# Natural row order with 8 KB runs, a quadrant move on TensorE, and a third held value pass, in an attention kernel fed from HBM

## The chip, the cores and the metric

The kernel runs on one core of one Trainium2 chip. The metric is the device time of one execution in microseconds (us), as the median of several runs. All runs quoted here are of the fast state and ran at a granted TensorE clock of 1.00. The experiments were timed in five batches on several chips (e1 to e4, e5 to e8, e9 to e12, e13 to e16, e17 and e18), each with the kernel before in the same rounds. Its median was 1242.7 to 1245.7 us in them, so medians of two batches can be off against each other by up to 3 us. A ratio is always to the kernel before of the same rounds, and is the safer number between batches.

## The reference, cut to what matters

```python
# x: 8 rows (batch elements) of 512; caches: 8 x 8 groups x 8192 tokens x 128; 32 query heads, 4 per group; all bf16
def _A_ref(x, k_cache, v_cache, wq, wo):
    q = (x @ wq) ...                      # 8 x 32 heads x 1 x 128
    scores = einsum("bhqd,bhkd->bhqk", q, k) * 128 ** -0.5
    p = softmax(scores)
    return einsum("bhqk,bhkd->bhqd", p, v) ... @ wo
def _B_ref(x, w1, w2):
    return silu(x @ w1) @ w2
x = A_x
x = x + _A_ref(_layernorm(x), A_k_cache, A_v_cache, A_wq, A_wo)    # layer 0
x = x + _B_ref(_layernorm(x), B_w1, B_w2)
x = x + _A_ref(_layernorm(x), A_k_cache, A_v_cache, A_wq, A_wo)    # layer 1, the same caches
x = x + _B_ref(_layernorm(x), B_w1, B_w2)
```

The keys and values of both layers are the same 268 MB. The kernel keeps the transposed keys of one batch element in SBUF for layer 1, so keys are read once and values twice: 402.7 MB, of 484.8 MB in all.

## The kernel before

A planner in Python simulates the engines, fixes the order of instructions and gives each load a place in a ring of ten 512 KB cells. Every load goes out from SyncE in that fixed order, and waits there until its cell is free. A "unit" is one layer, batch element and group: four key cells are transposed by VectorE in 32x32 blocks (1.99 us a cell), TensorE makes the scores, GpSimd and VectorE find the maximum over all tokens, ScalarE takes the exponential, and TensorE multiplies four value cells.

Between layer 0 and layer 1 of one batch element there is a chain without large loads: output projection, residual, feed-forward, norm, queries. The loads that wait for it stop the stream, because layer 1 can't score before its queries exist. So the value passes of the last two units of layer 1 are held back ("held", N_DEF) and done in the next such boundary, while layer 0 of the next element is interleaved too.

```python
N_GRAN = 11; N_P = 3; N_DEF = 2; N_BD = 4; T_TURN = 1.2
...
    def load_v(b, g, P):      # 128 partitions x 4096 B, one run each
        return load_gran(f"v{b}.{g}.{P}", v_src(b, g)[P], 1)
    def v_src(b, g):
        return A_v_cache[b, g].rearrange("(P n r) d -> P n (r d)", P=4, n=128)
    def load_k(b, g, c4):
        src = A_k_cache[b, g].rearrange("(p c4 cg) d -> c4 p (cg d)", p=128, c4=4)
        return load_gran(f"k{b}.{g}.{c4}", src[c4], 1)
...
    def turns(b, g):
        new = slot(g).bitcast(U32).rearrange("p (k i c4) -> p c4 k i", i=32, c4=4)   # output in 16 B steps
        for c4 in range(4):
            kn = load_k(b, g, c4)
            def turn(kn=kn, c4=c4):
                raw = gran(kn.give).bitcast(U32).rearrange("p (k j) -> p k j", j=32)
                op(dve, lambda: dve.transpose(new[:, c4], raw), ...)
...
        def exp():
            op(act, lambda: act.activation(pt[:, :], sv, ACT.Exp, scale=SM_SCALE), ...)
...
# norm: 1/sqrt(var) as a power on GpSimd, which otherwise runs partition_all_reduce
            op(pool, lambda: pool.tensor_tensor(rstd[:, 0:nb], var[:, 0:nb], expo[:, 0:nb], ALU.pow), ...)
...
            for h in held:                       # at the boundary between the layers
                values(h)
```

## Time and profile before

| | before |
|---|---|
| time, median of 4 runs | 1244.2 us (1241.7 to 1246.8) |
| profiled span | 1245.3 us |
| DMA queue of the inputs, share of 16 engines | 98.7% |
| TensorE, VectorE, ScalarE busy | 51%, 57%, 5% |
| bandwidth on its plateau | 408 GB/s |

These are lines of the profile's page: the span, busy times, the bandwidth in 40 equal slices, packets, the queue of instruction fetches (packets, MB, share), and two groups of instructions (line, engine, operation, output and input, count, busy us, mean ns of one, idle time just before them and what ended most of it).

```profile
span 1245.3 us, 45478 instructions
PE 631.6 (51%) x20640; PEld 593.0 (48%) x20640; DVE 708.4 (57%) x1236; ACT 63.0 (5%) x202; POOL 117.0 (9%) x295
...
GB/s 362 407 398 408 337 371 408 408 408 356 393 408 408 407 371 407 407 408 399 376 409 407 407 394 373 408 408 408 371 389 408 407 407 364 410 407 408 394 339 208
DMA packets 136865, 484.80 MB, mean 389 GB/s; under 512 B 14544, under 2 KB 20448, under 8 KB 136672
...
q8 instruction: 162, 2.65, 0.9%
...
L605 DVE STREAM_TRANSPOSE kts<-ring 128x1024 uint32<-128x1024 uint32 x256 | 503.2, 1988 | 116.6 <-DMA ring<-in_A_k_cache_dram 116.4
...
L656 PE MATMUL sc<-bd,kts 128*128 128x16 bf16 x8192 | 278.2, 174 | 160.7 <-issue 53.2
```

The bandwidth row is the one to read. It lies at 408 wherever nothing disturbs it and dips once per batch element. The dip of the third batch element in stretches of 10 us (columns: length, busy us and count of each engine, granted clock, DMA share, GB/s):

```profile
434.00:444.00 10.00, 4.75 (x156) 4.45 (x156) 8.30 (x14) 0.77 (x2) 1.39 (x4) 1.00 0.99 380
444.00:454.00 10.00, 4.15 (x145) 3.90 (x141) 4.44 (x6) 0.00 (x0) 0.50 (x2) 1.00 1.02 395
454.00:464.00 10.00, 6.02 (x200) 5.72 (x201) 7.71 (x13) 0.94 (x3) 1.10 (x3) 1.00 0.95 341
464.00:474.00 10.00, 4.58 (x155) 4.26 (x151) 5.87 (x10) 0.56 (x2) 1.17 (x3) 1.00 1.02 399
```

The share of busy DMA engines stays at 0.95 or more here while the bandwidth falls. Part of the loss thus shows as packets that take longer (up to 1.2 us for one of 4096 B) and not as idle engines.

And lines of the waits view (who waited, for what; us in total, times, longest): what SyncE's queue waited for before it could issue a load, and what TensorE and GpSimd waited for.

```profile
SPq L89 <- DVE kts L605: 270.6, 146, 8.2
SPq L89 <- PE ot L733: 252.9, 246, 4.8
...
PE ot L733 <- DMA ring<-in_A_v_cache_dram: 115.7, 123, 5.6
POOL rstd L413 <- issue: 7.1, 1, 7.1
```

SyncE waits in most of the span (779 us in all by that view), and far less than that is lost: up to ten cells can be in flight, and the row stays at 408 GB/s as long as a cell comes free in time. So a wait is counted as a loss only where the bandwidth falls.

A quantity that the rest uses is the **loss**: the span less the stream time. The stream time is every packet counted at what one of its size costs on the plateau (160.3 ns for 4096 B, read from undisturbed stretches; the packets of 4 B that go along are contained in these figures and not counted again), over 16 engines. For the kernel before it is 1187.6 us of stream and 57.7 us of loss.

### The profile page before, as it was taken

Reading aid. Unit: us, or ns where it says so; the run is one execution under the profiler, and the core shown is the slowest. Engines: PE = TensorE matmul, PEld = TensorE weight load, DVE = VectorE, ACT = ScalarE, POOL = GpSimd, SP = SyncE. Lnnn points to the kernel's source line nnn. Section 1 sums busy time; section 2 is a strip of 40 time slices with the busy share of each in tenths; the row PEclk is TensorE's granted clock in tenths of the full one; section 3 lists DMA queues with packets and bytes.
Section 4 is the critical chain, followed back from the end, with each engine's and each line's share of the span. In section 5 each row is a group of like instructions: output and inputs, shape, how many; then the busy total and the mean of one; then the engine's idle time right before and its main releaser. Section 6 shows DMA issues by size and latency. Waiting matters only on the chain.

```text
span 1245.3 us, 45478 instructions
## 1 busy us (share of the span) xinstructions
PE 631.6 (51%) x20640; PEld 593.0 (48%) x20640; DVE 708.4 (57%) x1236; ACT 63.0 (5%) x202; POOL 117.0 (9%) x295
## 2 busy tenths in 40 slices
PE   2334545455554654546454554555555455454555
PEld 2333545445543544545444454544545455444554
DVE  7745466826477265764557546574556826577221
ACT  0000000000000000000000000000000000000000
POOL 1000010101010010110000100110101101011010
DMA  9999999999999999999999999999999999999995
GB/s 362 407 398 408 337 371 408 408 408 356 393 408 408 407 371 407 407 408 399 376 409 407 407 394 373 408 408 408 371 389 408 407 407 364 410 407 408 394 339 208
DMA packets 136865, 484.80 MB, mean 389 GB/s; under 512 B 14544, under 2 KB 20448, under 8 KB 136672
## 3 DMA queue, kind: packets, MB, share of 16 engines
q1 hardware_dynamic: 136672, 481.90, 98.7%
q8 instruction: 162, 2.65, 0.9%
q14 instruction: 31, 0.25, 0.1%
HBM read 481.83 MB, written 0.01 MB: 387 GB/s over the span
## 4 chain that ended last, share of the span: by engine, by line
DMA 41%; DVE 25%; issue 20%; PE 10%; SPq 2%; POOL 2%; ACT 0%; POOLq 0%; DVEq 0%
DMA ring<-in_A_k_cache_dram 24%; DVE kts L605 19%; DMA ring<-in_A_v_cache_dram 10%; DMA ring<-in_A_wq_dram 7%; PE sc L656 5%; PE ot L733 2%; SPq L312 2%; DVE sc L678 2%; DVE small L668 2%; PE misc L563 1%; POOL small L673 1%; DVE small L687 1%; POOL small L692 1%; DVE bd L640 0%; PE yt L784 0%
## 5 line engine op out<-in xcount | busy, mean ns | idle before, releaser
L605 DVE STREAM_TRANSPOSE kts<-ring 128x1024 uint32<-128x1024 uint32 x256 | 503.2, 1988 | 116.6 <-DMA ring<-in_A_k_cache_dram 116.4
L733 PE MATMUL ot<-p,ring 128*128 128x4 bf16 x8192 | 287.4, 167 | 177.0 <-DMA ring<-in_A_v_cache_dram 115.7
L656 PE MATMUL sc<-bd,kts 128*128 128x16 bf16 x8192 | 278.2, 174 | 160.7 <-issue 53.2
L733 PEld LDWEIGHTS ot<-p,ring 128*128 128x128 bf16 x8192 | 255.5, 104 | 193.6 <-DMA ring<-in_A_v_cache_dram 131.1
L656 PEld LDWEIGHTS sc<-bd,kts 128*128 128x128 bf16 x8192 | 249.8, 104 | 168.9 <-issue 56.0
L673 POOL PARTITION_ALL_REDUCE small<-small x128 | 48.1, 376 | 728.9 <-DVE small L668 631.8
L668 DVE TENSOR_REDUCE small<-sc 128x4 f32<-128x256 f32 x128 | 51.9, 406 | 107.6 <-PE sc L656 107.4
L683 ACT ACTIVATE p<-sc 128x256 bf16<-128x256 f32 x128 | 49.0, 383 | 729.6 <-DVE sc L678 729.6
L784 PE MATMUL yt<-z,ring 128*128 128x4 bf16 x1024 | 36.8, 166 | 93.1 <-DVE z L762 89.8
L692 POOL PARTITION_ALL_REDUCE small<-small x128 | 55.0, 431 | 268.4 <-DVE small L687 266.1
L784 PEld LDWEIGHTS yt<-z,ring 128*128 128x128 bf16 x1024 | 33.0, 104 | 96.2 <-issue 96.0
L563 PE MATMUL misc<-xn,ring 128*128 128x1 bf16 (+1 forms) x1152 | 36.2, 166 | 68.7 <-DMA ring<-in_A_wq_dram 62.1
L563 PEld LDWEIGHTS misc<-xn,ring 128*128 128x128 bf16 x1152 | 33.8, 104 | 71.1 <-issue 64.9
L678 DVE TENSOR_TENSOR sc<-sc,small 128x256 f32<-128x256 f32 x128 | 57.1, 447 | 18.2 <-POOL small L673 17.9
L687 DVE TENSOR_REDUCE small<-p 128x4 f32<-128x256 bf16 x128 | 51.2, 401 | 21.3 <-ACT p L683 21.0
L632 PE MATMUL qx<-qab,sel 128*128 128x4 bf16 x256 | 16.6, 169 | 54.5 <-DVE bd L640 54.5
L696 DVE RECIPROCAL small<-small 128x4 f32<-128x4 f32 x128 | 21.6, 168 | 34.6 <-POOL small L692 34.6
L632 PEld LDWEIGHTS qx<-qab,sel 128*128 128x128 bf16 x256 | 11.8, 106 | 56.5 <-DVE bd L640 56.5
L640 DVE TENSOR_TENSOR bd<-qx,mask 128x64 bf16<-128x64 f32 x128 | 27.7, 217 | 16.2 <-PE qx L632 16.0
L571 DVE CAST qtb<-misc 128x4 bf16<-128x4 f32 (+1 forms) x32 | 5.3, 166 | 54.3 <-PE misc L563 54.3
L743 DVE TENSOR_TENSOR qab<-ot,small 128x4 bf16<-128x4 f32 x64 | 10.0, 157 | 43.6 <-PE ot L733 43.4
L762 DVE TENSOR_TENSOR z<-ot,small 128x16 bf16<-128x16 f32 x64 | 10.5, 164 | 37.7 <-PE ot L755 37.7
(61 smaller groups left out, 206.3 us busy)
## 6 DMA issues: line engine op xcount, KB each, us to landing
ring<-in_A_v_cache_dram SPq DMA_DIRECT2D x512, 512.0 KB, 10.8
ring<-in_A_k_cache_dram SPq DMA_DIRECT2D x256, 512.0 KB, 10.6
ring<-in_A_wq_dram SPq DMA_DIRECT2D x72, 512.0 KB, 10.8
ring<-in_A_wo_dram SPq DMA_DIRECT2D x64, 512.0 KB, 11.0
kts<-in_A_wo_dram SPq DMA_DIRECT2D x2, 2048.0 KB, 16.9
w<-in_B_w_dram SPq DMA_DIRECT2D x2, 1792.0 KB, 14.9
ring<-in_A_x_dram SPq DMA_DIRECT2D x1, 8.0 KB
out_dram<-ring SPq DMA_DIRECT2D x1, 8.0 KB
```

The costliest lines, as they stand in the source:

```text
L563: steps.append(lambda h=h, kt=kt, c=c: pe.matmul(qp[:, h * nb:(h + 1) * nb], gran(wn[kt].give)[:, c:c + DH], xn[:, b0:b0 + nb, kt], start= ...
L605: op(dve, lambda: dve.transpose(new[:, c4], raw), reads=[res("ring", kn.give)], writes=[res("kt", g)], add=(c4 > 0))
L632: steps.append(lambda fe=fe: pe.matmul(QX[:, R * fe:R * fe + R], sel[:, fe].rearrange("p a j -> p (a j)"), qsrc, start=True, stop=True))
L656: steps.append(lambda cg=cg, fe=fe: pe.matmul(sc[:, 16 * cg:16 * cg + 16], kv[:, cg, fe // 2, fe % 2], bd[:, 16 * fe:16 * fe + 16], start= ...
L668: op(dve, lambda: dve.tensor_reduce(mxp[sm], sv.rearrange("p (k h) -> p h k", h=R), AX.X, ALU.max), reads=[res(*scr)], writes=[res("mxp", ...
L673: op(pool, lambda: pool.partition_all_reduce(mxa[sm], mxp[sm], 128, bass.bass_isa.ReduceOp.max), reads=[res("mxp", sm)], writes=[res("mxa" ...
L678: op(dve, lambda: dve.tensor_tensor(v, v, mxa[sm].unsqueeze(1).to_broadcast([128, NCH, R]), ALU.subtract), reads=[res("mxa", sm)], writes= ...
L683: op(act, lambda: act.activation(pt[:, :], sv, ACT.Exp, scale=SM_SCALE), reads=[res(*scr)], writes=[res("p", sm)])
L687: op(dve, lambda: dve.tensor_reduce(ssm[sm], pt[:, :].rearrange("p (k h) -> p h k", h=R), AX.X, ALU.add), reads=[res("p", sm)], writes=[re ...
L692: op(pool, lambda: pool.partition_all_reduce(ssa[sm], ssm[sm], 128, bass.bass_isa.ReduceOp.add), reads=[res("ssm", sm)], writes=[res("ssa" ...
L733: steps.append(lambda cg=cg, k=k: pe.matmul(ot[:, 0:R], vt[:, cg, :], pt[:, k:k + R], start=(P == 0 and cg == 0), stop=(P == 3 and cg == N ...
L784: steps.append(lambda j=j, dt=dt: pe.matmul(YT[:, dt * R:(dt + 1) * R], w[:, j, dt * 128:(dt + 1) * 128], zt[:, R * j:R * j + R], start=(g ...
```

## The change

Its intent: let keys and values come in natural order, with 8192 B per partition instead of 4096 B, so that the DMA engines pay for half as many packets. Two cells then form a pair of 1 MiB that lands and comes free at once. In natural order the probability of a token sits, after the transposes, in another quadrant of 32 partitions than its value. So 16 small TensorE matmuls per unit against slices of the identity move the probabilities between quadrants, and ScalarE copies them back to SBUF. Beside that, the transposes write runs of 128 B, three value passes are held back instead of two, and the queries' weights for half the heads come after the first held pass. The exponentials get one buffer, and the masked queries two instead of four.

```diff
-N_DEF = 2
+N_DEF = 3
-N_BD = 4
+N_BD = 2
...
-    def load_k(b, g, c4):
-        src = A_k_cache[b, g].rearrange("(p c4 cg) d -> c4 p (cg d)", p=128, c4=4)
-        return load_gran(f"k{b}.{g}.{c4}", src[c4], 1)
+    def load_k(b, g, half):
+        src = A_k_cache[b, g].rearrange("(p hh y) d -> hh p (y d)", p=128, hh=2)
+        return load_cells(f"k{b}.{g}.{half}", 2, [(lambda buf: buf, src[half])])      # values alike
...
-        new = slot(g).bitcast(U32).rearrange("p (k i c4) -> p c4 k i", i=32, c4=4)
+        new = slot(g).bitcast(U32).rearrange("p (q ck f c4 i) -> p q ck c4 f i", q=4, f=2, i=32, c4=4)
...
         def exp():
-            op(act, lambda: act.activation(pt[:, :], sv, ACT.Exp, scale=SM_SCALE), ...)
+            op(act, lambda: act.activation(pe_out[:, :], sv, ACT.Exp, scale=SM_SCALE), ...)
+        def swap():
+            src = pe_out[:, :].rearrange("p (ck P h) -> p P ck h", ck=NCG, P=4)
+            new = sc[:, 256:512].rearrange("p (ck c4 h) -> p c4 ck h", ck=NCG, c4=4)
+            for c4 in range(4):
+                for P in range(4):
+                    steps.append(lambda c4=c4, P=P: pe.matmul(
+                        new[32 * P:32 * P + 32, c4], ident[:, 32 * c4:32 * c4 + 32], src[:, P], ...))
+        def back_in():
+            op(act, lambda: act.activation(pt[:, :], sc[:, 256:512], ACT.Copy), ...)
...
-            for h in held:
+            for k, h in enumerate(held):
+                if k == 1:
+                    second_q.update(queries(f"c{b}", prio, 0, b, 1, [ready]))
                 values(h)
```

Cut: the planner's handling of neighbouring cells, its new durations, and renamed helpers.

## The prediction

> **What bounds the kernel now.** The input stream. The page shows the DMA engines 99% busy, no compute engine above 57% (VectorE), and the bandwidth row at 407 to 410 GB/s wherever nothing disturbs it. 484.8 MB at that plateau of 408.7 GB/s are 1186 us of the 1245.3 us span. Reading the bandwidth in 4 us windows, I find the other 59 us as: about 4 at the start; about 32 in seven dips, one per batch element, 30 to 45 us wide (128-172, 280-324, 436-468, 584-620, 728-768, 876-916, 1024-1060); about 7 at 1176-1216; about 15 in the tail, after the last values have landed.

> **The packets.** A 4096 B packet takes 159 ns (the commonest duration), a 3584 B one 140 ns, a 1024 B one 46 ns: 36.8 ns per KB plus about 8.5 ns per packet. [...] For 8192 B I estimate 310 ns (the few 8192 B instruction-fetch packets show 309 at best), so the plateau goes from 409 to about 420 GB/s. Only keys and values change, 402.7 of the 484.8 MB: 985 us become 959. **Gain 26 us, all on the critical resource.**

> **The dips.** In the dip at 436-468, the second feed-forward norm ends at 424.7, the query matmuls wait until 427.5 for their weights, scores end near 433, the first probabilities come at 437. Meanwhile loaded values sit in the ring and SyncE waits (12 us for key transposes, 6 for value matmuls in this window). The change holds back three passes instead of two, and puts the query weights after the first: so 4 MiB of values, 10 us of stream, follow the weights and can be consumed without new probabilities. That is as long as the chain from weights landed to probabilities. I expect the seven dips to lose about 12 us instead of 32. **Gain 20 us.**

> **The transposes.** Each is 1.98 us for 1024 words, and one follows another every 1.9 us. Their output goes in steps of 16 B. [...] The new output has runs of 128 B[...] In mid-pass this gains nothing; in dips it frees key cells sooner.

> **What is added.** 128 groups of 16 matmuls (64 columns) on TensorE, about 0.6 us each by the 16-matmul groups here (0.57 us), and 128 ScalarE copies at about 0.38 us: +49 us ScalarE, some 60 us TensorE, both far from full. About 1.2 us more latency between exponentials and values; hidden in mid-pass, where units run one ahead. A single buffer for the exponentials and two masked-query buffers instead of four serialise a little.

> **The ring.** Ten cells become five pairs: 1 MiB lands and comes free at once, single cells fragment pairs. I charge 3 us. Start +1; tail unchanged.

> Sum: 1246 - 26 - 20 + 3 + 1, with some slack off: about 1202; faster transposes pull it slightly lower, to 1199 us, range 1180 to 1224. Chances: faster 0.88, same 0.09, slower 0.03.

> **Checks.** Packets of 8192 B at about 310 ns; plateau near 420 GB/s; [...]dips shallower; ScalarE near 110 us; SyncE's waits for key transposes (270 us) smaller.

> **What would make it wrong.** No faster plateau with 8 KB runs; pairs so coarse that the stream starves in mid-pass; transposes unchanged at 1.98 us (then key pairs are held 3.8 us); the quadrant matmuls slow, or blocking TensorE's in-order stream while ScalarE finishes.

What is cut had no trace behind it: a statement on the cost of output steps of 16 B, and the transposes' new time and VectorE's new busy time, which rested on it, here and in the checks (the faster transposes are what "this" and "it" in that paragraph mean); also a remark on the fixed cost per packet, for which the 8.5 ns read from the trace stand alone. The sum came to 1199 us: the terms that are written out give 1204, some slack made it 1202, and the last 3 us are for the faster transposes.

## The result, and the profile after

The kernel after takes 1229.9 us (1229.3 to 1234.0, 4 runs) against 1244.2 us: a ratio of 0.9892, with a 95% interval of 0.9858 to 0.9925. It is faster by 1.1%, not by 3.8%, and it lies outside the predicted range. (A ratio is the mean time of one kernel's fast runs over that of the other's of the same rounds, so not quite the ratio of the medians quoted.) Differences under 2% are called "same"; to "same" the prediction had given a chance of 0.09.

The same lines of the page for the kernel after, with the new quadrant matmuls as the last:

```profile
span 1227.8 us, 48979 instructions
PE 683.5 (56%) x22688; PEld 627.0 (51%) x22688; DVE 536.5 (44%) x1236; ACT 108.9 (9%) x330; POOL 117.1 (10%) x295
...
GB/s 371 416 405 417 272 403 419 416 390 417 409 417 408 385 419 416 415 404 367 417 399 417 415 393 417 406 403 373 420 416 403 412 368 408 412 417 401 383 370 186
DMA packets 81580, 485.00 MB, mean 395 GB/s; under 512 B 8400, under 2 KB 14304, under 8 KB 32224
...
q8 instruction: 178, 2.92, 0.9%
...
L627 DVE STREAM_TRANSPOSE kts<-ring 128x1024 uint32<-128x1024 uint32 x256 | 310.8, 1228 | 43.7 <-DMA ring<-in_A_k_cache_dram 43.1
...
L678 PE MATMUL sc<-bd,kts 128*128 128x16 bf16 x8192 | 275.6, 175 | 88.1 <-issue 59.0
...
L715 PE MATMUL sc<-expd,ident 128*32 128x64 bf16 x2048 | 54.0, 239 | 48.1 <-ACT expd L705 35.7
```

The plateau did rise, to 417 to 420. But the row is more ragged, and its fifth slice is at 272 where it was at 337. The dip of the third batch element, again in stretches of 10 us:

```profile
412.00:422.00 10.00, 7.28 (x264) 7.22 (x264) 2.22 (x11) 0.00 (x0) 0.94 (x2) 1.00 0.83 317
422.00:432.00 10.00, 5.64 (x188) 5.05 (x185) 4.25 (x12) 1.15 (x3) 1.24 (x3) 1.00 1.01 424
432.00:442.00 10.00, 6.27 (x213) 5.63 (x210) 5.19 (x12) 0.77 (x2) 0.74 (x2) 1.00 1.02 419
```

The old dip, 20 to 50 us after the residual (the addition of the output projection that ends layer 0's attention), is gone. A new one stands 10 to 20 us after it, while the last of the held value passes are being loaded. The waits:

```profile
SPq L89 <- PE ot L775: 429.3, 186, 8.2
SPq L89 <- DVE kts L627: 262.8, 101, 7.8
...
PE ot L775 <- DMA ring<-in_A_v_cache_dram: 202.1, 131, 6.4
POOL rstd L433 <- issue: 79.8, 8, 11.5
...
PE sc L678 <- issue: 59.0, 38, 3.1
```

Three things changed there. SyncE waits much more for value matmuls to give back a cell (429 against 253 us). TensorE waits more for values to land (202 against 116). And GpSimd's power of the norm now waits for "issue" eight times, nearly 10 us each (before, in seven of the eight boundaries, the wait ended with the variance). Such totals don't say what was lost: in e13 below, SyncE waits 461 us for value matmuls, and the loss is far smaller.

In the account of stream and loss: 1160.3 us of stream (27.3 less than before), but 67.4 us of loss (9.7 more). The loss by stretch, in us, from residual to residual of the eight batch elements:

| | start | seven boundaries and the passes after them | tail | sum |
|---|---|---|---|---|
| before | 3.9 | 8.6, 5.6, 3.4, 3.6, 4.2, 4.6, 3.8 | 20.1 | 57.7 |
| after | 3.7 | 12.3, 4.0, 3.6, 6.2, 5.0, 4.9, 6.2 | 21.6 | 67.4 |

So the question is why a loss that should have shrunk by about 20 us grew by 10.

### The profile page after: what moved, and what is told of

Read it like the earlier page. It is cut to its first block, busy times and chain, and to the rows that moved or that the text cites. A ratio compares the mean times of both kernels' runs of the same rounds, so it can differ in the third digit from the quotient of the medians.

```text
span 1227.8 us, 48979 instructions
## 1 busy us (share of the span) xinstructions
PE 683.5 (56%) x22688; PEld 627.0 (51%) x22688; DVE 536.5 (44%) x1236; ACT 108.9 (9%) x330; POOL 117.1 (10%) x295
## 4 chain that ended last, share of the span: by engine, by line
DMA 40%; issue 21%; PE 18%; DVE 15%; POOL 2%; SPq 2%; ACT 1%; POOLq 0%; DVEq 0%
DMA ring<-in_A_v_cache_dram 28%; DVE kts L627 9%; DMA ring<-in_A_k_cache_dram 9%; PE ot L775 6%; PE sc L678 5%; DMA ring<-in_A_wq_dram 3%; SPq L327 2%; PE misc L583 2%; DVE sc L700 2%; DVE small L690 1%; PE misc L485 1%; PE misc L467 1%; POOL small L695 1%; PE sc L715 1%; DVE small L725 1%
## 5 line engine op out<-in xcount | busy, mean ns | idle before, releaser
L775 PE MATMUL ot<-p,ring 128*128 128x4 bf16 x8192 | 283.2, 167 | 241.1 <-DMA ring<-in_A_v_cache_dram 202.1
L775 PEld LDWEIGHTS ot<-p,ring 128*128 128x128 bf16 x8192 | 252.7, 104 | 260.7 <-DMA ring<-in_A_v_cache_dram 214.6
L627 DVE STREAM_TRANSPOSE kts<-ring 128x1024 uint32<-128x1024 uint32 x256 | 310.8, 1228 | 43.7 <-DMA ring<-in_A_k_cache_dram 43.1
L705 ACT ACTIVATE expd<-sc 128x256 bf16<-128x256 f32 x128 | 48.9, 382 | 556.8 <-DVE sc L700 550.8
L715 PE MATMUL sc<-expd,ident 128*32 128x64 bf16 x2048 | 54.0, 239 | 48.1 <-ACT expd L705 35.7
L700 DVE TENSOR_TENSOR sc<-sc,small 128x256 f32<-128x256 f32 x128 | 54.0, 422 | 31.6 <-POOL small L695 31.6
L725 DVE TENSOR_REDUCE small<-expd 128x4 f32<-128x256 bf16 x128 | 51.2, 400 | 23.0 <-ACT expd L705 23.0
L715 PEld LDWEIGHTS sc<-expd,ident 128*32 128x32 bf16 x2048 | 31.9, 118 | 56.7 <-ACT expd L705 43.3
L794 ACT ACTIVATE attna<-ot 128x4 bf16<-128x4 f32 x64 | 11.1, 173 | 362.8 <-PE ot L775 362.8
## 6 DMA issues: line engine op xcount, KB each, us to landing
kts<-in_A_wo_dram SPq DMA_DIRECT2D x2, 2048.0 KB, 16.5
```

What stands on the lines that cost most here:

```text
L627: op(dve, lambda: dve.transpose(new[:, q], raw[:, c]), reads=cells_of(kn), writes=[res("kt", g)], add=(q > 0))
L700: op(dve, lambda: dve.tensor_tensor(v, v, mxa[sm].unsqueeze(1).to_broadcast([128, NCH, R]), ALU.subtract), reads=[res("mxa", sm)], writes= ...
L715: steps.append(lambda c4=c4, P=P: pe.matmul(new[32 * P:32 * P + 32, c4], ident[:, 32 * c4:32 * c4 + 32], src[:, P], start=True, stop=True))
L725: op(dve, lambda: dve.tensor_reduce(ssm[sm], pe_out[:, :].rearrange("p (k h) -> p h k", h=R), AX.X, ALU.add), reads=[res("expd")], writes= ...
L775: steps.append(lambda x=x, k=k: pe.matmul(ot[:, 0:R], vt[:, x, :], pt[:, k:k + R], start=(P == 0 and x == 0), stop=(P == 3 and x == NCG - 1)))
```

## The experiments

The theories, all open at the start: (T1) 8 KB runs don't gain in the stream what was estimated; (T2) the third held pass doesn't work; (T3) the path from exponentials to values got longer; (T4) the quadrant matmuls use TensorE time, or (T4b) TensorE instructions are short in supply; (T5) pairs of cells are too coarse; (T6) GpSimd's change of program at the norm became slower or exposed (so I call the gap between an all-reduce and the power, with two configuration instructions in it: 8.8 to 11.5 us in the kernel after). There were 18 runs. A caution for all of them: every run was told correct, even those that multiply values by probabilities of other tokens. So that verdict can't tell right from wrong here. Which results are right follows from the code, and is said each time.

### First round: the parts alone

**e1**, the kernel after, with each 1 MiB load as two DMAs of 4096 B packets. The result is right.

```diff
-        return load_cells(f"k{b}.{g}.{half}", 2, [(lambda buf: buf, src[half])])
+        return load_cells(f"k{b}.{g}.{half}", 2, [(lambda buf, k=k: buf[:, k * GR:(k + 1) * GR],
+            src[half][:, k * GR:(k + 1) * GR]) for k in range(2)])       # values alike
```

> The changed kernel with each 1 MiB load split into two DMAs of 4096 B packets; ring, order and arithmetic unchanged. Theory R (the 8192 B packets gave exactly the stream gain and nothing else): the stream costs 26 us more, so about 1256 us. Theory S (long packets also slow the GpSimd program switch before the first feed-forward norm: 8.8 to 11.5 us in the changed kernel, 7.1 to 7.9 us in the one before): switches fall back to about 7.5 us, the dips after a batch shrink, and the time is near 1244 us.

Measured: 1252.6 us (ratio 1.0068), 22.7 us slower than the kernel after. In the traces an 8192 B packet takes 309 ns and a 4096 B packet 159 ns. T1 falls: the stream's gain is as estimated. So does the expectation's second theory, that long packets slow GpSimd's change of program: with 4096 B packets, the four changes that stick out in e1's trace still took 9.0 to 12.2 us. (In the kernel before they took up to 8.6 us, not 7.9.) And the rest of the change, without it, makes the kernel slower than before.

**e2**, the kernel before, with the third held pass and the query weights behind the first.

```diff
-N_DEF = 2
+N_DEF = 3
-            for h in held:
+            for k, h in enumerate(held):
+                if k == 1:
+                    second_q.update(queries(f"c{b}", prio, 0, b, 1, [ready]))
-                    if g % 4 == 0:
+                    if g % 4 == 0 and g >= (4 if held else 0):
```

> The kernel before with three value passes held back and the query weights behind the first of them, nothing else. Theory H (holding back works; the pairs of cells spoil it in the changed kernel): the loss of about 4 us per batch, 15 to 50 us after the residual, goes and no new dip comes: about 1225 us. Rival (holding back itself moves the dip to 10 to 20 us after the residual, where the query weights and values wait in the ring for the feed-forward chain): 1240 us or more.

**e3**, the kernel after with two held passes.

```diff
-N_DEF = 3
+N_DEF = 2
```

> The changed kernel with two held passes instead of three. If the third held pass brings in the changed kernel what I predicted (20 us), it takes about 1250 us; if the third pass only moves the dip, it stays within 5 us of 1230 us.

Measured: e2 1231.3 us (0.9896), e3 1235.3 us (0.9929). In the kernel before, the third pass takes the loss from 57.7 to 42.7 us: T2 falls as well, though 15 us is not the 20 predicted. The bandwidth row of e2's page shows it:

```profile
GB/s 362 408 398 408 328 378 407 407 408 407 403 407 408 388 408 400 407 408 395 407 400 408 407 389 408 403 407 399 402 407 403 408 393 403 404 406 406 395 367 203
```

In the kernel after it is worth only 5 us, and the ranges of the two ratios overlap. So these few lines alone give nearly the time of the whole change, and the long runs' 27 us must have been given back somewhere.

**e4**, the kernel after without quadrant matmuls and without the copy back, planned anew. The result is wrong.

```diff
-            op(act, lambda: act.activation(pe_out[:, :], sv, ACT.Exp, scale=SM_SCALE), ...)
+            op(act, lambda: act.activation(pt[:, :], sv, ACT.Exp, scale=SM_SCALE), ...)
-        m4 = plan.add(f"sw{u}", "PE", 0.6, swap, pr - 2, [n4])
-        n4 = plan.add(f"bk{u}", "ACT", 0.42, back_in, pr, [m4] + p_users.get(sm, []))
```

> The changed kernel without the quadrant matmuls and the copy back (a wrong result on purpose: probabilities stay in the wrong quadrants). If their latency or their place in TensorE's order costs time, about 1222 us; if they are hidden as predicted, 1230 us within 2 us.

Measured: 1214.0 us (0.9759), 16 us faster than the kernel after, with a loss of 54.7 us. The added work was not free.

### Second round: what of the added work costs

**e5** is e4 with the order and the cells of the kernel after kept (the two steps stay in the plan and emit nothing). **e6** keeps the matmuls, on the finished probabilities, with nobody waiting for the result. **e7** has no matmuls, but a ScalarE copy in their place, and then the copy back, so that the path is about as long. All three are wrong.

```diff
 e5:  -  m4 = plan.add(f"sw{u}", "PE", 0.6, swap, pr - 2, [n4])
      +  m4 = plan.add(f"sw{u}", "PE", 0.6, lambda: None, pr - 2, [n4])      # back_in alike
 e6:  -  src = pe_out[:, :].rearrange("p (ck P h) -> p P ck h", ck=NCG, P=4)
      +  src = pt[:, :].rearrange("p (ck P h) -> p P ck h", ck=NCG, P=4)     # and no copy back
 e7:  +  op(act, lambda: act.activation(sc[:, 256:512], pe_out[:, :], ACT.Copy), ...)   # instead of swap
```

> The changed kernel without the quadrant matmuls and the copy back, but with each engine's order and all ring cells exactly as in the changed kernel (wrong result on purpose). Theory L (what the matmuls and their latency cost on the chip is the 16 us): about 1214 us, like the run without them that was planned anew. Rival P (the other plan, made without them, was the gain): about 1229 us.

> The changed kernel with the 16 quadrant matmuls per unit still run, but on a copy that nobody uses: the values no longer wait for them and the copy back is gone (wrong result on purpose). Theory B (TensorE executes in order and stands still at these matmuls until ScalarE has finished): about 1228 us. Theory T (the cost is that the probabilities come later, so values lie longer in the ring): about 1215 us.

> The changed kernel with the 16 matmuls replaced by one ScalarE copy of the same length in time (wrong result on purpose): the probabilities come as late as before, TensorE has nothing to do with it. Theory B: about 1216 us. Theory T: about 1228 us.

Measured: e5 1216.4 us (0.9769), e6 1224.6 us (0.9844), e7 1217.0 us (0.9779). The order of the plan matters little here (e5 is 2.4 us from e4). The longer path alone costs 0.6 us over e5, which is within the scatter: T3 falls for a delay of this size. TensorE's work alone, with nobody waiting for it, costs 8 of the 13 us; the other 5 were not split further, and e6 was also planned anew. TensorE does run in order, as theory B supposes: in the trace of the kernel after all 22,688 matmuls start in the order of the program, and before the quadrant matmuls TensorE stood idle for 35.7 us in all until an exponential was done.

**e8** gave only the planner another duration (3.4 instead of 0.6 us) for the first norm's root, to let it plan for T6.

```diff
-        r = plan.add(f"{tag}.root", "POOL", 0.6, root, prio, [v])
+        r = plan.add(f"{tag}.root", "POOL", 3.4 if tag[-4:] != ".ln2" else 0.6, root, prio, [v])
```

> The changed kernel, where only the planner's duration of the first norm's root on GpSimd is 3.4 us instead of 0.6 (the trace shows 1.1 to 3.9 us of waiting for the program switch). Instructions are the same, their order and the ring cells differ. If the dip 10 to 20 us after the residual comes from an order planned for a chain that is in fact longer, it shrinks: about 1220 us. If the chain itself is the limit, nothing changes: 1230 us.

Measured: 1224.8 us (0.9843), but from 1219.6 to 1229.8, and the profiled run lost as much as the kernel after (67.8 us). It is inconclusive. (Another order of the same instructions may thus move the median by some 5 us.)

### Third round: time on TensorE, or instructions

**e9** and **e10** are e5 with dummy matmuls on constants, which wait for nothing and which nothing uses, among the score matmuls of each unit: 16 of the quadrant matmuls' shape (e9), or 4 of 256 columns (e10), which keep TensorE busy longer with a quarter of the instructions. Wrong, as e5.

```diff
+                if q == 1:
+                    for k in range(16):                                   # e9
+                        steps.append(lambda k=k: pe.matmul(sc[32 * (k % 4):32 * (k % 4) + 32, 256:320],
+                            ident[:, 32 * (k // 4):32 * (k // 4) + 32], ident[:, 0:64], start=True, stop=True))
+                    for k in range(4):                                    # e10
+                        steps.append(lambda: pe.matmul(sc[:, 256:512], ident[:, :],
+                            ident[:, :].unsqueeze(1).to_broadcast([128, 2, 128]), start=True, stop=True))
```

> The same-plan kernel without the quadrant matmuls, with 16 matmuls of the same shape per unit that read a constant, wait for nothing and that nobody uses, put among the score matmuls. The traces show that TensorE stands still only at every 256th instruction, 6.1 us after the last such point, until a 16 KB instruction packet has landed. Theory F (the cost of the quadrant matmuls is that 4096 more TensorE instructions come in 16 more such packets): about 1225 us, 178 packets, some 50 us more standing still. Theory B (the cost is waiting in order for ScalarE): about 1216 us.

> As the run with 16 matmuls, but 4 matmuls of 256 columns per unit: about the same TensorE time in a quarter of the instructions. Theory F: about 1217 us (4 more packets instead of 16). If plain TensorE time is the cost: about 1225 us, like the run with 16.

Measured: e9 1232.3 us (0.9909), e10 1219.1 us (0.9807). Busy times on the page, and the scores' waits for "issue" in the waits view, for e5, e9 and e10 in turn:

```profile
PE 629.8 (52%) x20640; PEld 590.8 (49%) x20640; DVE 536.1 (44%) x1236; ACT 57.8 (5%) x202; POOL 117.1 (10%) x295
...
PE sc L678 <- issue: 30.4, 22, 3.2
```

```profile
PE 684.1 (56%) x22688; PEld 632.1 (51%) x22688; DVE 536.2 (44%) x1236; ACT 57.9 (5%) x202; POOL 117.1 (10%) x295
...
PE sc L683 <- issue: 51.6, 38, 2.9
```

```profile
PE 732.8 (60%) x21152; PEld 665.3 (55%) x21152; DVE 535.8 (44%) x1236; ACT 59.1 (5%) x202; POOL 117.1 (10%) x295
...
PE sc L683 <- issue: 28.7, 24, 3.0
```

e10 added 103 us of TensorE time and cost 2.6 us. e9 added 54 us of it (so about half, where the expectation had them alike), with four times as many instructions, and cost 15.8 us. (By the ratios, as e5 is of another batch, it is 5 us for e10 and 17 for e9.) So it is the number of instructions that costs and not the time: T4 falls and T4b stands. (The two dummies also differ in the width of their tiles, 32 against 128 columns, which was not varied alone.) The sum of the pauses over 0.3 us at block borders is 76 us in e5, 138 in e9, 60 in e10 and 129 in the kernel after, there at some 80 of 178 borders (worked out from the trace's times; a recount comes within some 15 us, depending on which gap is taken at a border). The pauses alone don't tell the cost: by the recount that gives 115 for the kernel after, the kernel before, without quadrant matmuls, has 108. What counts is how many of them are absorbed.

**e11** moves the probabilities another way: 16 ScalarE exponentials per unit, of 32 partitions each, write straight into the new quadrants. The result is right.

```diff
+            for k, (c4, P) in enumerate((c4, P) for c4 in range(4) for P in range(4)):
+                op(act, lambda c4=c4, P=P: act.activation(dst[32 * P:32 * P + 32, c4],
+                    src[32 * c4:32 * c4 + 32, P], ACT.Exp, scale=SM_SCALE), ...)
```

> The changed kernel with the exponentials written straight to their new quadrants by 16 ScalarE pieces of 32 partitions (right result); no quadrant matmuls, no copy back. [...] Theory F with cheap latency: about 1218 us, faster than the changed kernel. If latency is what costs: 1230 us or more.

Measured: 1269.8 us (1.0218).

```profile
L708 ACT ACTIVATE p<-sc 32x64 bf16<-32x64 f32 x2048 | 439.3, 214 | 448.5 <-DVE sc L700 401.5
```

Sixteen pieces of 214 ns are 3.4 us on the path where one exponential was 0.38, and in that trace TensorE's value matmuls waited 197 us for probabilities. A path longer by some 3 us (by 2 us than that of the kernel after, where a median of 1.04 us lies between the end of an exponential of 0.38 us and the end of its copy back) is not hidden (though e11's order was planned anew as well); in e7 a smaller delay, two ScalarE operations of 0.38 us, cost nothing that can be told from scatter.

**e12** takes the power off GpSimd: an inverse square root on VectorE, by a bit trick and two Newton steps, for the norms of one row. The result is right, to rounding.

```diff
+            dve.tensor_scalar(y.bitcast(I32), v.bitcast(I32), 1, None, op0=ALU.arith_shift_right)
+            dve.tensor_scalar(y.bitcast(I32), y.bitcast(I32), -1.0, 1597463007.0, op0=ALU.mult, op1=ALU.add)
+            # then twice y = y * (1.5 - v / 2 * y * y)
-        r = plan.add(f"{tag}.root", "POOL", 0.6, root, prio, [v])
+        r = (plan.add(f"{tag}.root", "DVE", 1.3, root1, prio, [v]) if nb == 1 else ...)
```

> The changed kernel with the reciprocal root of the one-row norms on VectorE (a bit trick and two Newton steps), so GpSimd never switches programs within the stream. If the switch (1.1 to 3.9 us of waiting per batch, 16 us in all) is on the path of the dip 10 to 20 us after the residual: about 1218 us. If the ring's space is the limit: 1229 us.

Measured: 1224.4 us (0.9843), 5.5 us faster than the kernel after. GpSimd alternates between the all-reduce and the power, and at each change the trace has a pair of configuration instructions (MODIFY_POOL_CONFIG; 38 in the kernel after, for 18 changes and the start). In the traces of the kernel after, GpSimd stands still for 8.8 to 11.5 us at the change to the power, of which 1.1 to 3.9 us stick out behind the variance in each of eight norms (16.5 us in all). In the kernel before it is 7.1 to 8.6 us, but in seven of eight cases the wait for the variance ended it, so that the change may have been done sooner; in the eighth it took 7.1. Why it takes longer in the kernel after is open. T6 stands, at about 5 us; not all that sticks out was lost.

### Fourth round: the size of a load, and versions that might win

By then T5 had not been tried. **e13** is the kernel after with each cell loaded and freed alone, in 4096 B runs; natural order, quadrant matmuls and fast transposes are kept, and the result is right. It differs from e1, which has the same packets and the same work, in the granularity (and in the order that the planner then chooses).

```diff
-        src = A_k_cache[b, g].rearrange("(p hh y) d -> hh p (y d)", p=128, hh=2)
-        return load_cells(f"k{b}.{g}.{half}", 2, [(lambda buf: buf, src[half])])
+        src = A_k_cache[b, g].rearrange("(p q y) d -> q p (y d)", p=128, q=4)
+        return load_cells(f"k{b}.{g}.{q}", 1, [(lambda buf: buf, src[q])])      # values alike; freed one by one
```

> The after kernel with every key and value cell loaded and freed alone again (4096 B runs, natural order and quadrant matmuls kept). To be set beside e1 (the same packets and the same matmuls, loaded in 1 MiB pairs: 1252.6 us). If pairs cost the 3 us that the prediction charged: about 1249 us. If pairs are the large missing loss, 10 us or more: about 1241 us. If they cost nothing: 1252 us.

Measured: 1234.8 us (0.9922), against 1252.6 us (1.0068) for e1. By the ratios pairs cost 0.0146 of 1244 us, 18 us; by the losses of the profiled runs 14 us (45.3 against 59.6). T5 is probably the largest of all, and larger than in the expectation's high case (1241 us). The same place in both traces, 10 to 20 us after the third element's residual, and TensorE's waits for values; first e13, then e1:

```profile
416.00:426.00 10.00, 8.40 (x287) 8.11 (x288) 1.85 (x9) 0.00 (x0) 0.48 (x2) 1.00 1.00 385
...
PE ot L773 <- DMA ring<-in_A_v_cache_dram: 138.5, 155, 4.9
```

```profile
419.00:429.00 10.00, 7.22 (x257) 7.08 (x258) 1.31 (x6) 0.00 (x0) 0.39 (x1) 1.00 0.80 271
...
PE ot L777 <- DMA ring<-in_A_v_cache_dram: 238.6, 146, 5.7
```

With the same packets and the same instructions, the stream of the pairs falls to 271 GB/s where that of the single cells stays at 385, and TensorE waits 100 us longer for values to land: by the code it may touch no half of a pair before both are there. (Whether the landing, the giving back or the finding of two neighbouring free cells costs most was not split.)

**e16** puts e9's 16 dummy matmuls into e2, whose ring is of single cells. The result is right.

```diff
 e2 with
+                if q == 1:
+                    for k in range(16):
+                        steps.append(lambda k=k: pe.matmul(...))          # as in e9
```

> The before kernel with three held passes (e2: 1231.3 us) and 16 dummy matmuls per unit on constants, which wait for nothing and which nothing uses. If the supply of TensorE instructions costs about 1 us per 256 whatever the layout: about 1246 us. If that cost belongs to the after kernel's pairs and order alone: 1231 us.

Measured: 1240.0 us (0.9974), 8.7 us over e2. Both expectations miss: the supply of instructions costs in this layout too, about half of what it cost e9 in pairs (15.8 us), and as much as it cost e6 (8 us). The pauses are there in full, 215 us of them. The whole of e13 is only 3.5 us over e2, though it has the quadrant matmuls; its transposes are faster, which may have paid for part.

**e14** is e12 with the expansion of the queries done for several groups at once: 320 matmuls fewer than the kernel after, right result.

```diff
+            qall = qab[:, b, cols] if layer == 0 else qtb[:, cols]       # one, three or four groups
             for fe in range(4):
-                    QX[:, R * fe:R * fe + R], sel[:, fe]..., qsrc, start=True, stop=True))
+                    qx[:, fe, cols], sel[:, fe]..., qall, start=True, stop=True))
```

> The after kernel with e12's root on VectorE, and with the expansion of the queries done for several groups at once: some 700 TensorE matmuls fewer, right result. If TensorE instructions cost about 1 us for each 128 matmuls (256 with their weight loads), it is about 4 us below e12 (1224.4): about 1220 us. If only the time that the matmuls occupy TensorE counts, it is at 1224 us, as those matmuls are short.

Measured: 1223.3 us (0.9833, interval 0.9812 to 0.9854), 1.1 us under e12. That can't be told from nothing; the expectation had also counted more matmuls saved (some 700) than the page shows (22,688 to 22,368). Those matmuls are short, 169 ns each in the kernel after, 33 us for all 512. It is the fastest kernel with a right result, 0.5% under the kernel after.

**e15**, **e17** and **e18** tried to keep 8 KB runs for the keys alone, two neighbouring quarters of the old order at a time, where no quadrant has to be changed. All have e14's other parts, and right results. e15 has the old transposes. e17 orders the tokens so that transposes are fast, and loads the values into that order. e18 also takes value cells in pairs.

```diff
 e15: -  new = slot(g)...rearrange("p (q ck f c4 i) -> p q ck c4 f i", ...)
      +  new = slot(g)...rearrange("p (k i c4) -> p c4 k i", i=32, c4=4)     # keys in pairs, values single, no swap
 e17: +  new = slot(g)...rearrange("p (k c4 i) -> p c4 k i", i=32, c4=4)
      +  src = A_v_cache[b, g].rearrange("(P i c4 r) d -> P c4 i (r d)", P=4, i=32, c4=4)
 e18: +  load_cells(f"v{b}.{g}.{P}", 2, [... src[P + k] ... for k in range(2)])
```

> 8 KB runs for the keys alone, two neighbouring quarters of the old order at a time (no other row order, so the probabilities are already in the right quadrants: no quadrant matmuls, no copy back); values in 4 KB cells as before; three held passes, root on VectorE, batched expansion, four masked-query buffers. Right result. Stream time is half way between the two, about 1174 us; with losses like those of before with three held passes (42.7 us) less the switch (4) it is about 1213 us; with losses like those of the after kernel without the quadrant matmuls (55) it is about 1229 us.

> As e15 (keys in 8 KB runs and pairs of cells, values in single 4 KB cells, no quadrant matmuls, root on VectorE, batched expansion), but the tokens of a chunk are ordered so that the transposes write runs of 128 B, and the values are loaded in that order of partitions, still 4 KB a run. Right result. If e15 lost its time to the 1.97 us transposes that hold the key pairs: losses fall from 83 to about 45 us, 1222 us in all, or less. If it lost it because single cells and pairs fragment one ring: it stays above 1240 us.

> As e17, but values also take their cells in pairs (two 4 KB runs a partition, given back together). If pairs as such cost 14 to 18 us, it is as much slower than e17, some 1235 us. If fragmentation of the ring by singles is what costs, it is faster than e17, near 1220 us.

Measured: e15 1263.1 us (1.0150), a loss of 83 us. Its transposes and SyncE's waits for them:

```profile
L644 DVE STREAM_TRANSPOSE kts<-ring 128x1024 uint32<-128x1024 uint32 x256 | 492.5, 1974 | 7.6 <-DMA ring<-in_A_k_cache_dram 7.6
...
SPq L89 <- DVE kts L644: 387.4, 113, 6.7
```

A pair of keys stays in the ring for two transposes of 1.97 us. Whether that or the mixture of single cells and pairs was the harm, e17 was to tell, and it failed for another reason: e17 took 3437 us (2.76) and e18 3441 us (2.77). A stretch of e17 in which values alone were loaded:

```profile
1030.00:1040.00 10.00, 2.79 (x96) 2.70 (x96) 0.86 (x2) 0.00 (x0) 0.37 (x1) 1.00 0.26 106
```

The DMA engines are 26% busy, which is about four packets of 4096 B in flight at a time instead of 16, and the stream is at 106 GB/s. The slowest dimension of the new source is 4; in e15, where it is 128, the stream of keys and values together runs at 317 to 414 GB/s in nine stretches of 16 us. I take the 4 for the cause, but that was not shown: no run changed it alone. That source was a mistake, and the question of e17 and e18 stays open. One thing e17 does show: beside e15, where the transposes read the cells alike, only the order of their output differs (16 B steps in e15, runs of 128 B here), and the mean falls from 1974 to 1229 ns.

```profile
L645 DVE STREAM_TRANSPOSE kts<-ring 128x1024 uint32<-128x1024 uint32 x256 | 310.5, 1229 | 101.4 <-DMA ring<-in_A_k_cache_dram 100.6
```

## Why the prediction was wrong, point by point

The way from before to after in steps that were run, in medians and in stream plus loss of the profiled runs:

| step | run | us | stream | loss |
|---|---|---|---|---|
| before | before | 1244.2 | 1187.6 | 57.7 |
| third held pass | e2 | 1231.3 | 1187.6 | 42.7 |
| natural order, quadrant matmuls, fast transposes, fewer buffers, new planner durations, cells single | e13 | 1234.8 | 1188.3 | 45.3 |
| cells in pairs | e1 | 1252.6 | 1188.3 | 59.6 |
| 8 KB runs | after | 1229.9 | 1160.3 | 67.4 |

Where the losses lie, in us, summed over the seven boundaries (worked out from the packets' times in the traces; start and tail are left out):

| run | 0 to 20 us after the residual | 20 to 50 us after it | the passes after that | sum |
|---|---|---|---|---|
| before | 5 | 26 | 2 | 33 |
| e2: third held pass | 11 | 5 | 5 | 21 |
| e13: cells single | 8 | 7 | 6 | 22 |
| e1: cells in pairs | 24 | 3 | 7 | 33 |
| after | 26 | 3 | 13 | 42 |
| e3: after, two held passes | 26 | 13 | 8 | 47 |
| e5: after, no quadrant matmuls | 23 | 2 | 7 | 32 |
| e9: e5 and 16 dummy matmuls | 21 | 7 | 15 | 43 |

The step that failed is thus the forecast for the boundaries: dips that lose 12 us instead of 32, with 3 us charged for the ring of pairs and nothing for TensorE. The third held pass did take the old dip away (26 to 5 us), but the seven boundaries lost 42 us and not 12, because the coarse pairs opened a new dip in the first 20 us (8 to 24 us, e13 to e1), and the many short matmuls cost more in the passes.

- **"Gain 26 us, all on the critical resource": right.** 27.3 us of stream time; 309 ns per 8192 B packet against an estimate of 310. For each packet dropped 2 x 159 - 309 = 9 ns were saved. But 22.7 us of it arrived, and the loss rose by 8; probably because a faster stream leaves the same chains of compute less time, which no run isolates.
- **"Gain 20 us" from the dips: mechanism right, size off.** e2 shows 13 us in time and 15 in loss. In the kernel after it was worth about 5 (e3): there the later dip lost only 13 us with two held passes, and the new early dip is the same with two as with three (26 us), so the third pass neither caused nor filled it. Even the 5 us are doubtful, as most of the difference in loss (17.0 against 12.3 us) lies in the first boundary, which has no held passes.
- **"I charge 3 us" for the ring of pairs: this is the step that failed most.** It measured 14 to 18 us (e13 against e1). Nearly all of that lies in the first 20 us after a residual (8 us in e13, 24 in e1), not in mid-pass, where the prediction looked for it. It named coarse pairs as what could make it wrong, and still charged them like a rounding error.
- **TensorE and ScalarE "both far from full"; "about 1.2 us more latency ... hidden in mid-pass": half right, and the wrong half mattered.** ScalarE's load (109 us, predicted 110) and the latency (1.04 us in the median; e7) cost nothing that the runs can tell. But the quadrant matmuls cost 13 us in pairs (after against e5), and dummies that wait for nothing cost as much (e9). TensorE's instructions arrive in blocks of 256, typically not faster than one in 6 us (6.2 in the median at the borders with a pause, in the kernel after), and 4096 more of them cost where the matmuls already come that fast. Busy share doesn't show that; pauses for "issue" at every 256th instruction do, though the kernel before has nearly as many.
- **The start "+1; tail unchanged": small.** The start lost 3.7 us against 3.9, the tail 21.6 against 20.1. But the first boundary, which has no held passes, lost 12.3 us instead of 8.6. In the windows from 126 to 130 us the stream is at 4 GB/s, and in the kernel before it still ran at 283 GB/s from 128 to 132.
- **Faster transposes: right.** They took 1.23 us (1.99 before); the estimate that the prediction gave is cut, as no trace was behind it. 16 B steps cost 0.76 us more for 1024 words than runs of 128 B (0.75 between e15 and e17, where nothing else about them differs). That "faster transposes pull it slightly lower" was not seen, and "SyncE's waits for key transposes (270 us) smaller" is hardly so (263).
- **Not in the prediction at all:** GpSimd's change of program, about 5 us (e12).

Pairs and instruction supply may not be independent. 16 more matmuls cost 8.7 us over e2, with single cells, and 8 to 16 us in pairs (e6, after and e9 over e5). If there is a difference, a reason could be that a pause of 2 us on TensorE delays the return of one cell in one case and of two in the other, while the ring holds ten cells or five pairs. That is argued, not shown: no run changed the ring's depth, and with e6 the ranges meet. Nor was it settled how much of the 14 to 18 us came from the planner's other order of loads; where the order alone was changed, the median moved by 2 us (e4, e5) and 5 us (e8).

## What to carry to other kernels

When a transfer is made longer to save packets, count what the buffer loses in granularity before counting the saving: here 27 us of stream were bought with 14 to 18 us, because 512 KB cells became 1 MiB pairs. Before adding many tiny TensorE instructions, look at waits for "issue" and at the packets on the instruction queue, not at the busy share: here 512 long matmuls with 103 us of TensorE time cost 3 to 5 us, and 2048 short ones with 54 us cost 16 to 17. And try the cheapest part of a change alone: a few lines (e2) gave nearly the whole gain of this change.
